# Matmul operands read alternately from two halves, in a kernel of pooled attention and two FFNs

## The chip, the cores and the metric

One core of one Trainium2 chip runs the whole program. The metric is device time in microseconds (us). Five engines work side by side: TensorE (PE; its weight loads are shown as PEld), VectorE (DVE), ScalarE (ACT), GpSimd (POOL) and SyncE (SP), which issues most of the DMAs.

## The reference

`q` is 2 x 12288 x 128, `kv` is 2 x 384 x 32 x 128, and each FFN has weights of 128 x 2048 and 2048 x 128.

```python
kv_pool = kv.reshape(B, H // 4, 4, W // 4, 4, C).mean(axis=(2, 4))   # 768 keys per batch
k = v = kv_pool.reshape(B, -1, C) @ w_sr
s = (q @ k.transpose(0, 2, 1)) / sqrt(C)
a = softmax(s)
x = (a @ v).reshape(B * 12288, C)
h = x @ moe_w_in;  x = where(h > 0, h, exp(min(h, 0)) - 1) @ moe_w_out
h = maximum(x @ moe2_w_in, 0);  out = (h * h) @ moe2_w_out
```

All of it is float32.

## The kernel before, in words

The 24,576 tokens are worked off in 48 blocks of 512 (`NB`), 24 for each batch. Channels lie on the partitions and tokens along the row, so a block is the moving operand of nearly every matmul, 512 columns wide, and weights are the stationary one. Each FFN has 16 chunks of 128 hidden channels (`NF`). For full precision each operand is held as a high part and a low part (`xH`, `xL`; `wi0H`, `wi0L`), and one product takes three matmuls: weight low by operand high, high by high, high by low (`products`, lines 308 to 310).

A block t goes through these steps:

- **scores** (lines 684 to 690): four pieces of 128 tokens. The queries stand still, the keys `kH`, `kL` of the batch move, 768 columns in spans of 512 and 256. Row maximum on DVE (L707), exponential on ACT (L711), normalisation on ACT or POOL, then a 32x32 transpose on DVE (`turn`, L729) and 16 DMAs (`move`, L791) that finish the transposition into `pL`.
- **values** (`weigh`, lines 807 to 811): `pH` is cut off by ACT (L801), `pL` by DVE (L805), and six key chunks of three matmuls each give x. Blocks 0 to 2 do this with single-part operands and 128-wide matmuls (`plain_values`, L833).
- **hidden** 0 and 1 (L880): x or y against 16 weight chunks into PSUM banks. FFN 0 then has exp on ACT (L891), `less_one` on POOL (L894), `pick` on DVE (L898), the high part on ACT (L902), the low part on DVE (`gL`, L905). FFN 1 has relu and square on ACT (L923, L926), the high part on POOL (L929), the low part on DVE (`sL`, L933).
- **down** 0 and 1 (L947): the hidden channels in pairs of chunks, 16 products summed in one bank. y is split by ACT and DVE (`split`, L620, L621); the output of FFN 1 is transposed on DVE (L969) and written by four DMAs (L974), each taking 32 channels.

Matmul results lie in the order in which the moving operand is read. Before the change everything is read in the order in which it lies, and token columns stay in their order from q to the output.

The order of all instructions on all engines is made in advance by `Program.order`. Each step has an engine, a cost and a priority (its due time, in blocks of 16 x 3200). The planner walks through the costs as times, and at each point takes from an engine's queue the step that can start first, with preference by priority. After 130,000 ns of planned time costs are multiplied by `SLACK` of the engine. The table `MOVED` shifts the priority of single steps. A step's cost thus sets the order and no more; each engine on the chip works through its list and waits on semaphores.

Of the kernel before, what the change touches and what calls it, by code (L numbers as in the profile page):

```python
# [22 lines left out]
IDLE, MARGIN, FILLER, COLD, WARM = 330.0, 60.0, 224.0, 430.0, 6300.0  # L23
OPENING, EAGER = 60000.0, 250.0
BULK = 130000.0
SLACK = {"pe": 1.0, "act": 1.17, "dve": 1.1, "pool": 1.16, "sp": 1.0}
LATENCY = {"pe": 197, "act": 135, "dve": 110, "pool": 120, "sp": 2300}
SAME = {"pe": 0, "act": 110, "dve": 0, "pool": 60, "sp": 2300}
BEGIN = {"pe": 1360.0, "act": 2500.0, "dve": 900.0, "pool": 1300.0, "sp": 1800.0}

MOVED = {
    "aH": {(0, 0, 3): 3720, (0, 2, 6): 28360, (1, 1, 5): 1580},
    "aL": {(0, 2, 2): 200, (0, 3, 1): 22430, (1, 1, 3): 2340},
    "cut": {(0, 0, 1): 12280, (0, 1, 1): 18660, (1, 1, 3): 17420},
    "down": {(0, 0, 10): -7210, (0, 0, 11): -61170, (0, 0, 9): -390, (0, 1, 11): 1860, (0, 2, 3): 17140,
        (0, 2, 9): 14060, (0, 3, 0): 4990, (0, 3, 8): -7760, (1, 0, 0): -34230, (1, 0, 11): 8280, (1, 0, 2): -28660,
        (1, 1, 2): 360, (1, 1, 3): -12810},
    "exp": {(0, 5): 9510, (0, 6): 7700, (1, 14): 10480, (2, 1): 1790, (3, 12): 55960, (3, 13): 8500},
    "hidden": {(0, 0, 12): -20, (0, 0, 8): 6730, (0, 1, 13): -3490, (0, 1, 15): -360, (0, 1, 6): 7080,
# [6 lines left out]
    "high_part": {(0, 1, 0): 11700, (1, 1, 2): 20980, (1, 1, 3): 9580},  # L46
    "join": {(1, 0, 2): -10420, (1, 1, 3): -28280},
    "k_hi": {(0, 1): -90},
    "less_one": {(3, 10): -10910, (3, 14): 17140},
    "low_part": {(1, 0, 1): 18510},  # L50
    "normalise": {(3, 0): 520, (4, 2): 4360},
    "pick": {(1, 11): 12410, (2, 0): 18920, (2, 3): -14380, (2, 6): -13180, (3, 10): -8840},
    "q_transpose": {(2,): -3420},
    "recip": {(3, 3): -2180},
    "relu": {(0, 3): -10730, (0, 7): -410, (1, 15): 11630, (1, 6): -29110, (2, 8): -3270},
    "scores": {(3, 1): 4220, (4, 3): -3470},
    "turn": {(4, 1): 11280},
    "v_hi": {(0,): 24340},
    "values": {(1, 3): -13460, (2, 1): 18540, (2, 3): 7470, (3, 2): 15850},
    "xL": {(3,): -2040},  # L60
    "yH": {(3,): -19030},
}


class Program:
# [25 lines left out]

    def order(self, kinds, fill=None):

        for tag, moved in MOVED.items():
            for key, by in moved.items():
                engine, cost, priority, *rest = self.ops[(tag, *key)]
                self.ops[(tag, *key)] = (engine, cost, priority + by, *rest)
# [77 lines left out]
def kernel(  # L175
# [19 lines left out]
    nc = tc.nc  # L195
# [107 lines left out]
    def f32(t):  # L303
        return t.bitcast(F32)

    def products(dst, lhs, rhs, start=True, stop=True):

        nc.tensor.matmul(dst, lhs[1], rhs[0], start=start, stop=False)  # L308
        nc.tensor.matmul(dst, lhs[0], rhs[0], start=False, stop=False)  # L309
        nc.tensor.matmul(dst, lhs[0], rhs[1], start=False, stop=stop)  # L310
# [209 lines left out]
    def make_keys(b, due):  # L520
# [20 lines left out]
        def make(x, due):  # L541
            ps, hi, lo = (x + "ps", b), (x + "H", b), (x + "L", b)
            scale = SCALE if x == "k" else 1.0

            def chunk(c):
                dst = v_chunk(flat(buf(*ps)), c)
                keys = buf("pooled", b)[:, c * P:(c + 1) * P]
                nc.tensor.matmul(dst, *((wsr, keys) if x == "k" else (keys, wsr)), start=True, stop=True)  # L548

            def hi_half(h):  # L550
                x = spans[h]
                nc.scalar.activation(buf(*hi)[:, x], flat(buf(*ps))[:, x], AF.Copy, scale=scale)

            def lo_half(h):
                x = spans[h]
                nc.vector.scalar_tensor_tensor(
                    out=buf(*lo)[:, x], in0=flat(buf(*ps))[:, x], scalar=scale, in1=f32(buf(*hi)[:, x]),
                    op0=ALU.mult, op1=ALU.subtract,
                )

            if b == 0:
                from_near(x, due)
            for c in range(NKC if b else 0):
                op((x, b, c), "pe", 280 if x == "k" else 223, due, partial(chunk, c),
                   kept + ([(x, b, 0)] if c else []),
                   [] if c else [("scores", ps), (x + "H", hi), (x + "L", lo)],
                   last=[("pooled", b)])
            if x == "v" and b == 0:
                plain_v(due)
                return  # L570
            for h in range(2):
                op((x + "_hi", b, h), "act", 370, due, partial(hi_half, h),
                   [(x, b, h)] if b == 0 else [(x, b, c) for c in range(4 * h, min(4 * h + 4, NKC))])
                op((x + "_lo", b, h), "dve", 470, due, partial(lo_half, h), [(x + "_hi", b, h)], last=[ps])
# [22 lines left out]

    spans = (slice(0, NB), slice(NB, NKEY))

    def v_chunk(x, c):  # L600
        return x[:, c * C:(c + 1) * C]

# [3 lines left out]
    G = P // 32  # L606
    q_rows = q.rearrange("b (t g j) c -> (b t) j g c", g=NB // 32, j=32)
    q_tokens = q.rearrange("b (t s p) c -> (b t) p s c", s=NS, p=P)
    out_rows = out.rearrange("(t g j) c -> t j g c", g=NB // 32, j=32)

    def pieces(x, a):
        return x[32 * a:32 * (a + 1), :].rearrange("p (g i) -> p g i", i=32)
# [14 lines left out]
    def attention(t, base):  # L627
# [53 lines left out]
        def softmax(s, due):  # L681
            k = (t, s)

            def scores():
                x = [a[:, s * P:(s + 1) * P] for a in parts("qT", t)]
                ps, kH, kL = flat(buf("scores", *k)), buf("kH", b), buf("kL", b)
                for y in spans:
                    nc.tensor.matmul(ps[:, y], x[0], kH[:, y], start=True, stop=False)  # L688
                    nc.tensor.matmul(ps[:, y], x[0], kL[:, y], start=False, stop=False)  # L689
                    nc.tensor.matmul(ps[:, y], x[1], kH[:, y], start=False, stop=True)  # L690

            def span_scores(h):
                x, y = [a[:, s * P:(s + 1) * P] for a in parts("qT", t)], spans[h]
# [102 lines left out]
        def weigh(j, due):  # L796
# [10 lines left out]
            def values():  # L807
                vH, vL = buf("vH", b), buf("vL", b)
                for i in range(2 * j, 2 * j + 2):
                    products(buf("xps", t), (v_chunk(vH, i), v_chunk(vL, i)),  # L810
                             [buf(x, t)[:, i, :] for x in ("pH", "pL")], start=(i == 0), stop=(i == NKC - 1))

            if t >= EARLY:
                op(("p_hi", *k), "act", 945, due, p_hi, [("move", t)] + ([("p_hi", t, 0)] if j else []),
# [3 lines left out]
            if j == NKC // 2 - 1:  # L818
                done = [("pH", t), ("pL", t)]
                if t % BPB == BPB - 1:  # L820
                    done += [("vH", b), ("vL", b)]
            op(("values", *k), "pe", 1364, due, values,
               ([("p_lo", *k)] if t >= EARLY else [("p_lo", t, s) for s in range(NS)])
               + ([("v_lo", b)] if b == 0 else [("v_lo", b, 0), ("v_lo", b, 1)]) + ([("values", t, j - 1)] if j else []),
               [("bank" if t > 2 else "bank0", ("xps", t))] if j == 0 else (), last=done)
# [49 lines left out]
    def hidden(j, t, i, due):  # L875
# [1 line left out]
        x = "xy"[j]  # L877

        def fn():
            products(buf("h", *k), [w[:, i, :] for w in wi[j]], parts(x, t))  # L880

        op(("hidden", *k), "pe", 682, due, fn, [(x + "L", t), ("low_part", j, 0, i // 4)], [("bank" if t + j > 2 else "bank0", ("h", *k))],
           last=[(x + "H", t), (x + "L", t)])

    def elu(t, i, due):
# [57 lines left out]
    def down(j, t, i, due):  # L943
        pair = (j, t, i // 2)

        def fn():
            products(buf("acc", j, t), [w[:, i, :] for w in wo[j]], [buf(x, *pair)[:, i % 2, :] for x in ("aH", "aL")],  # L947
                     start=(i == 0), stop=(i == NF - 1))

        def half(h):  # L950
            x = slice(h * NB // 2, (h + 1) * NB // 2)
            products(buf("acc", j, t, h)[:, :NB // 2], [w[:, i, :] for w in wo[j]],
                     [buf(y, *pair)[:, i % 2, x] for y in ("aH", "aL")], start=(i == 0), stop=(i == NF - 1))

        after = [("aL", *pair), ("low_part", j, 1, i // 4)]
        if t == NBLK - 1 and j:
# [2 lines left out]
                   after + ([("down", j, t, i - 1, h)] if i else []),  # L959
                   () if i else [("bank", ("acc", j, t, h))], last=[("aH", *pair), ("aL", *pair)])  # L960
            return
        op(("down", j, t, i), "pe", 682, due, fn, after + ([("down", j, t, i - 1)] if i else []),
           () if i else [("bank" if t + j > 2 else "bank0", ("acc", j, t))], last=[("aH", *pair), ("aL", *pair)])

    def store(t, due):
# [3 lines left out]
            nc.vector.transpose(out=buf("o", t), in_=buf(*acc))  # L969

        def write():
            for a in range(G):
                queue = nc.scalar if t == NBLK - 1 and a % 2 else nc.sync
                queue.dma_start(out=out_rows[t, :, :, 32 * a:32 * (a + 1)], in_=pieces(buf("o", t), a))  # L974
# [15 lines left out]
                op(("o_write", t, h), "sp", 1000, due, partial(write_half, h), [("o_transpose", t, h)], last=[("o", t)])  # L990
            return
        op(("o_transpose", t), "dve", 630, due, transpose, [("down", 1, t, NF - 1)], [("o", ("o", t))], last=[acc])
        op(("o_write", t), "sp", 2000, due, write, [("o_transpose", t)], last=[("o", t)])


    for t in range(NKC):
# [72 lines left out]
```

## Time and profile before

| what | value |
|---|---|
| median of 3 runs | 2542.16 us (2542.04 to 2542.49) |
| the profiled execution | 2542.52 us, of which the span of the trace is 2540.7 us |
| busy PE / DVE / ACT / POOL | 2531.9 / 2231.3 / 2080.5 / 1308.0 us |
| granted TensorE clock | 1.00 of full speed over the span |

Matmuls are pipelined: a matmul's duration in the trace (390 ns for 512 columns) overlaps the next one's, so the rate is read from the distance between two starts. The span of one execution is some 1.8 us shorter than its time.

### The profile page before, as it was taken

The numbers are of one execution on the slowest core, as the hardware profiler recorded it, in microseconds if no ns is written. First come the engines' busy times: TensorE is split into PE (matmuls) and PEld (weight loads), VectorE is DVE, ScalarE is ACT, GpSimd is POOL, SyncE is SP. The second block draws the span as 40 slices with busy tenths as digits, with TensorE's granted clock in tenths as the row PEclk, the third lists the DMA queues.
The fourth block names the chain that finished last, engine by engine and source line by source line (L and its number), as shares of the span: only waits on it lengthen the run. The fifth ranks groups of instructions, "written<-read, shape, count | busy, mean of one in ns | idle before, by whom it ended". The sixth has DMA issues, their size and how long they took to land.

```text
span 2540.7 us, 34933 instructions
## 1 busy us (share of the span) xinstructions
PE 2531.9 (100%) x11639; PEld 2107.5 (83%) x11639; DVE 2231.3 (88%) x2725; ACT 2080.5 (82%) x3137; POOL 1308.0 (51%) x1319
## 2 busy tenths in 40 slices
PE   9999999999999999999999999999999999999999
PEld 8888888888888888888888888888888888888888
DVE  7988889889898898988898888888888989888885
ACT  6988888788888788787888888888888888888886
POOL 4654454555665455554545445554555444544553
PEclk9999999999999999999999999999999999999999
DMA  6122111222122221221112111121112111211110
GB/s 225 38 48 49 34 38 34 55 59 46 42 46 61 56 46 42 63 51 34 38 34 56 41 38 34 45 51 34 38 34 60 37 38 34 49 44 31 33 30 13
DMA packets 358853, 119.28 MB, mean 47 GB/s; under 512 B 208912, under 2 KB 352912, under 8 KB 358672
## 3 DMA queue, kind: packets, MB, share of 16 engines
q1 hardware_dynamic: 357440, 116.85, 19.2%
q8 instruction: 92, 1.51, 0.2%
q14 instruction: 89, 0.73, 0.1%
q10 hardware_dynamic: 1232, 0.20, 0.0%
HBM read 33.61 MB, written 12.58 MB: 18 GB/s over the span
## 4 chain that ended last, share of the span: by engine, by line
PE 98%; DVE 1%; DMA 0%; ACT 0%; issue 0%; SPq 0%; DVEq 0%
PE banks L308 30%; PE banks L309 30%; PE banks L310 30%; PE banks L690 3%; PE banks L689 3%; PE banks L688 3%; PE banks L833 0%; DMA gH<-in_kv_dram 0%; PE banks L462 0%; DVE sL L933 0%; PE banks L736 0%; DVE gL L905 0%; DVE g L898 0%; DVE max L707 0%; PE banks L548 0%
## 5 line engine op out<-in xcount | busy, mean ns | idle before, releaser
L894 POOL TENSOR_SCALAR e<-e 128x512 f32<-128x512 f32 x768 | 706.4, 928 | 528.9 <-ACT e L891 441.3
L929 POOL TENSOR_SCALAR sH<-r 128x1024 fp32r<-128x1024 f32 x380 | 420.0, 1105 | 628.5 <-ACT r L926 256.3
L891 ACT ACTIVATE e<-banks 128x512 f32<-128x512 f32 x768 | 459.1, 600 | 196.7 <-PE banks L310 180.3
L933 DVE TENSOR_TENSOR sL<-r,sH 128x1024 fp32r<-128x1024 f32 x380 | 550.7, 1449 | 59.5 <-POOL sH L929 59.4
L905 DVE TENSOR_TENSOR gL<-g,gH 128x1024 fp32r<-128x1024 f32 x384 | 518.2, 1351 | 77.3 <-ACT gH L902 74.4
L923 ACT ACTIVATE r<-banks 128x512 f32<-128x512 f32 x768 | 458.9, 599 | 113.9 <-PE banks L310 98.8
L898 DVE SCALAR_TENSOR_TENSOR g<-e,banks 128x512 f32<-128x512 f32 x768 | 501.3, 671 | 24.0 <-POOL e L894 20.8
L902 ACT CAST gH<-g 128x1024 fp32r<-128x1024 f32 x384 | 401.9, 1047 | 14.2 <-DVE g L898 10.5
L926 ACT ACTIVATE r<-r 128x1024 f32<-128x1024 f32 x384 | 407.7, 1062 | 6.9
L308 PE MATMUL banks<-yH,wi1L 128*128 128x512 f32 x768 | 300.1, 391 | 0.2
L308 PE MATMUL banks<-xH,wi0L 128*128 128x512 f32 x768 | 300.1, 391 | 0.0
L308 PE MATMUL banks<-gH,wo0L 128*128 128x512 f32 x768 | 299.7, 390 | 0.0
L309 PE MATMUL banks<-yH,wi1H 128*128 128x512 f32 x768 | 299.4, 390 | 0.0
L309 PE MATMUL banks<-gH,wo0H 128*128 128x512 f32 x768 | 299.4, 390 | 0.0
L309 PE MATMUL banks<-xH,wi0H 128*128 128x512 f32 x768 | 299.2, 390 | 0.0
L310 PE MATMUL banks<-xL,wi0H 128*128 128x512 f32 x768 | 298.9, 389 | 0.0
L310 PE MATMUL banks<-yL,wi1H 128*128 128x512 f32 x768 | 298.8, 389 | 0.0
L310 PE MATMUL banks<-gL,wo0H 128*128 128x512 f32 x768 | 298.8, 389 | 0.0
L310 PE MATMUL banks<-sL,wo1H 128*128 128x512 f32 (+1 forms) x768 | 297.4, 387 | 1.0 <-DVE sL L933 1.0
L308 PE MATMUL banks<-sH,wo1L 128*128 128x512 f32 (+1 forms) x768 | 297.8, 388 | 0.0
L309 PE MATMUL banks<-sH,wo1H 128*128 128x512 f32 (+1 forms) x768 | 297.4, 387 | 0.0
L711 ACT ACTIVATE prob<-banks,max 128x768 f32<-128x768 f32 x191 | 172.3, 902 | 49.5 <-DVE max L707 46.4
(181 smaller groups left out, 4327.9 us busy)
## 6 DMA issues: line engine op xcount, KB each, us to landing
pL<-turned SPq DMA_DIRECT2D x720, 96.0 KB, 2.2
out_dram<-o SPq DMA_DIRECT2D x188, 64.0 KB, 1.9
q<-in_q_dram SPq DMA_DIRECT2D x180, 64.0 KB, 2.3
ld<-in_kv_dram SPq DMA_DIRECT2D x24, 256.0 KB, 3.6
ld<-in_kv_dram SPq DMA_DIRECT2D x4, 512.0 KB, 5.5
g<-in_kv_dram SPq DMA_DIRECT2D x4, 512.0 KB, 6.3
gH<-in_kv_dram SPq DMA_DIRECT2D x3, 512.0 KB, 7.8
r<-in_moe_w_in_dram SPq DMA_DIRECT2D x3, 511.8 KB, 6.9
```

Of the source, the lines that this page charges most:

```text
L308: nc.tensor.matmul(dst, lhs[1], rhs[0], start=start, stop=False)
L309: nc.tensor.matmul(dst, lhs[0], rhs[0], start=False, stop=False)
L310: nc.tensor.matmul(dst, lhs[0], rhs[1], start=False, stop=stop)
L891: nc.scalar.activation(buf("e", *k), buf(*h), AF.Exp)
L894: nc.gpsimd.tensor_scalar(out=buf("e", *k), in0=buf("e", *k), scalar1=-1.0, scalar2=1.0, op0=ALU.add, op1=ALU.mult)
L898: nc.vector.scalar_tensor_tensor(out=buf("g", *pair)[:, i % 2, :], in0=buf("e", *k), scalar=0.0, in1=buf(*h), op0=ALU.min, op1=ALU.max)
L902: nc.scalar.copy(buf("aH", 0, *pair), buf("g", *pair))
L905: nc.vector.tensor_sub(buf("aL", 0, *pair), buf("g", *pair), f32(buf("aH", 0, *pair)))
L923: nc.scalar.activation(buf("r", *pair)[:, i % 2, :], buf(*h), AF.Relu)
L926: nc.scalar.activation(buf("r", *pair), buf("r", *pair), AF.Square)
L929: nc.gpsimd.tensor_scalar(out=buf("aH", 1, *pair), in0=buf("r", *pair), scalar1=1.0, scalar2=1.0, op0=ALU.mult, op1=ALU.mult)
L933: nc.vector.tensor_sub(buf("aL", 1, *pair), buf("r", *pair), f32(buf("aH", 1, *pair)))
```

## The change

Every FFN product and every value product of the blocks from 3 on now reads its moving operand through `paired`: columns 0, 256, 1, 257, and so on, so two neighbouring reads lie 256 columns (1024 bytes) apart. The result lies in the order read. Values, hidden 0, down 0, hidden 1 and down 1 each shuffle the tokens once, and the write to memory takes the accumulated order into account (`out_rows`; blocks 0 to 2, whose values aren't shuffled, use `out_early` and eight DMAs instead of four).

The score matmuls read their keys alternately too: in batch 0 within each span (256 apart in the span of 512, 128 apart in that of 256), in batch 1 over all 768 columns, 384 apart. `kH` and `kL` are written in such places that the scores come out in the old order.

In the planner the cost of a hidden or down step goes from 682 to 648 and that of a value step from 1364 to 1296. `SLACK` is lowered for DVE and POOL, a new table `AFTER` shifts whole kinds of steps in the blocks from 3 on, and `MOVED` has other entries. So the order changes on every engine.

```diff
-SLACK = {"pe": 1.0, "act": 1.17, "dve": 1.1, "pool": 1.16, "sp": 1.0}
+SLACK = {"pe": 1.0, "act": 1.17, "dve": 1.085, "pool": 1.09, "sp": 1.0}
+AFTER = {("aH", 1): 8560, ("aL", 0): 1530, ("aL", 1): -9360, ("down", 1): -1890, "exp": -5170,
+         ("hidden", 0): 520, ("hidden", 1): 500, "less_one": 4410, "o_transpose": -5280, "p_hi": 10050,
+         "p_lo": -1040, "pick": -2620, "recip": -3590, "scores": -6800, "turn": 25890, "xL": 7740}
 MOVED = {
-    "aH": {(0, 0, 3): 3720, (0, 2, 6): 28360, (1, 1, 5): 1580},
+    "aH": {(1, 1, 0): 12060, (1, 1, 1): 5250},
...
     def order(self, kinds, fill=None):
+        for name, (engine, cost, priority, *rest) in self.ops.items():
+            if priority > -9e5 and len(name) <= 4:
+                staged = name[0] in ("hidden", "down", "aH", "aL")
+                block = name[1 + staged] if len(name) > 1 + staged else 0
+                if block >= 3:
+                    priority += AFTER.get(name[:2] if staged else name[0], 0)
+                    self.ops[name] = (engine, cost, priority, *rest)
...
+    def paired(x):
+        return x.rearrange("p (a b) -> p b a", a=2)
...
+            def place(y, h):
+                return of_span(b, y, h) if x == "k" else two(y[:, spans[h]])
             def hi_half(h):
-                nc.scalar.activation(buf(*hi)[:, x], flat(buf(*ps))[:, x], AF.Copy, scale=scale)
+                nc.scalar.activation(place(buf(*hi), h), two(flat(buf(*ps))[:, spans[h]]), AF.Copy, scale=scale)
...
+    def of_span(b, x, h):
+        if b:
+            return paired(x)[:, NB // 2 * h:min(NB // 2 * (h + 1), NKEY // 2), :]
+        return paired(x[:, spans[h]])
+
+    def two(x):
+        return x.rearrange("p (b a) -> p b a", a=2)
...
-    out_rows = out.rearrange("(t g j) c -> t j g c", g=NB // 32, j=32)
+    out_rows = out.rearrange("(t j g) c -> t j g c", g=NB // 32, j=32)
+    out_early = out.rearrange("(t k g e) c -> t e k g c", g=NB // 32, k=16, e=2)
...
-                for y in spans:
-                    nc.tensor.matmul(ps[:, y], x[0], kH[:, y], start=True, stop=False)
-                    nc.tensor.matmul(ps[:, y], x[0], kL[:, y], start=False, stop=False)
-                    nc.tensor.matmul(ps[:, y], x[1], kH[:, y], start=False, stop=True)
+                for h, y in enumerate(spans):
+                    hi, lo = of_span(b, kH, h), of_span(b, kL, h)
+                    nc.tensor.matmul(ps[:, y], x[0], hi, start=True, stop=False)
+                    nc.tensor.matmul(ps[:, y], x[0], lo, start=False, stop=False)
+                    nc.tensor.matmul(ps[:, y], x[1], hi, start=False, stop=True)
...
                     products(buf("xps", t), (v_chunk(vH, i), v_chunk(vL, i)),
-                             [buf(x, t)[:, i, :] for x in ("pH", "pL")], start=(i == 0), stop=(i == NKC - 1))
+                             [paired(buf(x, t)[:, i, :]) for x in ("pH", "pL")], start=(i == 0), stop=(i == NKC - 1))
...
-            products(buf("h", *k), [w[:, i, :] for w in wi[j]], parts(x, t))
-        op(("hidden", *k), "pe", 682, due, fn, [(x + "L", t), ("low_part", j, 0, i // 4)], [("bank" if t + j > 2 else "bank0", ("h", *k))],
+            products(buf("h", *k), [w[:, i, :] for w in wi[j]], [paired(y) for y in parts(x, t)])
+        op(("hidden", *k), "pe", 648, due, fn, [(x + "L", t), ("low_part", j, 0, i // 4)], [("bank" if t + j > 2 else "bank0", ("h", *k))],
...
-            products(buf("acc", j, t), [w[:, i, :] for w in wo[j]], [buf(x, *pair)[:, i % 2, :] for x in ("aH", "aL")],
+            products(buf("acc", j, t), [w[:, i, :] for w in wo[j]], [paired(buf(x, *pair)[:, i % 2, :]) for x in ("aH", "aL")],
...
+            if t < PLAIN:
+                for a in range(G):
+                    for e in range(2):
+                        nc.sync.dma_start(out=out_early[t, e, :, :, 32 * a:32 * (a + 1)],
+                                          in_=pieces(buf("o", t), a)[16 * e:16 * (e + 1)])
+                return
```

On TensorE, where a block's values begin (block 24 of 48; `turned` and `pL` are its weights' high and low part, `kH` and `kL` the keys), before:

```order
L688 MATMUL banks<-kH_11602,qTH_12954 128x256
L689 MATMUL banks<-kL_11603,qTH_12954 128x256
L690 MATMUL banks<-kH_11602,qTL_13010 128x256
L308 MATMUL banks<-turned_13097,vL_11669 128x512
L309 MATMUL banks<-turned_13097,vH_11668 128x512
L310 MATMUL banks<-pL_12965,vH_11668 128x512
```

and at the last two values of the same block, after the change:

```order
L323 MATMUL banks<-turned_13108,vL_11734 128x512
L324 MATMUL banks<-turned_13108,vH_11733 128x512
L325 MATMUL banks<-pL_12956,vH_11733 128x512
L323 MATMUL banks<-yH_12925,wi1L 128x512
L324 MATMUL banks<-yH_12925,wi1H 128x512
L325 MATMUL banks<-yL_12936,wi1H 128x512
L323 MATMUL banks<-xH_12727,wi0L 128x512
L324 MATMUL banks<-xH_12727,wi0H 128x512
L325 MATMUL banks<-xL_12765,wi0H 128x512
L714 MATMUL banks<-kH_11629,qTH_12880 128x512
L715 MATMUL banks<-kL_11630,qTH_12880 128x512
L716 MATMUL banks<-kH_11629,qTL_13027 128x512
```

Before, a block's six value triples stand in one piece behind the scores; now they come two by two, with hidden and down products and a score step between them.

On VectorE at the same place (`pL` is the low part of the value weights, `gL` and `sL` those of the two FFNs), before:

```order
L933 TENSOR_TENSOR sL_13107<-r_13032,sH_13084 128x1024
L805 TENSOR_TENSOR pL_12965<-pL_12965,turned_13097 128x1024 x2
L905 TENSOR_TENSOR gL_13137<-g_13077,gH_13105 128x1024
L805 TENSOR_TENSOR pL_12965<-pL_12965,turned_13097 128x1024
L707 TENSOR_REDUCE max_13150<-banks 128x1
```

and now:

```order
L831 TENSOR_TENSOR pL_12956<-pL_12956,turned_13108 128x1024
L959 TENSOR_TENSOR sL_13138<-r_13050,sH_13115 128x1024
L931 TENSOR_TENSOR gL_13151<-g_13076,gH_13122 128x1024
L831 TENSOR_TENSOR pL_12956<-pL_12956,turned_13108 128x1024
L733 TENSOR_REDUCE max_13166<-banks 128x1
L924 SCALAR_TENSOR_TENSOR g_13120<-e_13132,banks 128x512
L831 TENSOR_TENSOR pL_12956<-pL_12956,turned_13108 128x1024
L959 TENSOR_TENSOR sL_13198<-r_13103,sH_13177 128x1024
L931 TENSOR_TENSOR gL_13209<-g_13120,gH_13186 128x1024
```

The three `pL` steps stood close together and now have a pair of FFN steps between them; `sL` and `gL` come one behind the other.

## Rows read from the trace of the kernel before

**Rows 1.** The page's span and its busy times with shares and instruction counts.

```profile
span 2540.7 us, 34933 instructions
PE 2531.9 (100%) x11639; PEld 2107.5 (83%) x11639; DVE 2231.3 (88%) x2725; ACT 2080.5 (82%) x3137; POOL 1308.0 (51%) x1319
```

**Rows 2.** The page's chain that ended last, shares by engine.

```profile
PE 98%; DVE 1%; DMA 0%; ACT 0%; issue 0%; SPq 0%; DVEq 0%
```

**Rows 3.** All waits of PE: for whom, us in total, times, longest.

```profile
PE banks L1031 <- POOL ident masks.py:199: 1.4, 1, 1.4
PE banks L688 <- DVE turned L746: 1.1, 1, 1.1
PE banks L310 <- DVE sL L933: 1.0, 1, 1.0
...
PE banks L833 <- DVE turned L746: 0.2, 1, 0.2
```

**Rows 4.** PE's timeline by start (us): FFN matmuls, then scores.

```profile
1395.81 0.39 PE L308 MATMUL banks<-gH,wo0L 128*128 128x512 f32 x1
1396.04 0.39 PE L309 MATMUL banks<-gH,wo0H 128*128 128x512 f32 x1
1396.27 0.39 PE L310 MATMUL banks<-gL,wo0H 128*128 128x512 f32 x1
...
1403.29 0.39 PE L688 MATMUL banks<-kH,qTH 128*128 128x512 f32 x1
...
1403.97 0.28 PE L688 MATMUL banks<-kH,qTH 128*128 128x256 f32 x1
...
1404.33 0.40 PE L308 MATMUL banks<-turned,vL 128*128 128x512 f32 x1
```

**Rows 5.** PE's groups by line and form: count, busy, mean ns.

```profile
L308 PE MATMUL banks<-xH,wi0L 128*128 128x512 f32 x768 | 300.1, 391 | 0.0
L310 PE MATMUL banks<-sL,wo1H 128*128 128x512 f32 x752 | 292.9, 389 | 1.0 <-DVE sL L933 1.0
L308 PE MATMUL banks<-turned,vL 128*128 128x512 f32 x270 | 105.8, 392 | 0.0
L688 PE MATMUL banks<-kH,qTH 128*128 128x512 f32 x188 | 73.6, 392 | 1.1 <-DVE turned L746 1.1
L688 PE MATMUL banks<-kH,qTH 128*128 128x256 f32 x188 | 52.2, 278 | 0.0
```

**Rows 6.** A stretch of 200 us: busy and counts by engine, then clock, DMA.

```profile
core 0: us, PE busy (x) PEld busy (x) DVE busy (x) ACT busy (x) POOL busy (x), PEclk, DMA share, GB/s
1400.00:1600.00 200.00, 200.00 (x906) 166.30 (x904) 179.87 (x219) 166.16 (x250) 97.68 (x99) 1.00 0.17 38
```

**Rows 7.** PE's timeline in the opening: two matmuls in plain float32.

```profile
16.82 1.02 PE L658 MATMUL banks<-qT,red 128*128 128x512 f32 x2
17.68 0.38 PE L462 MATMUL banks<-o,g 128*128 128x128 f32 x2
```

**Rows 8.** DVE's groups by line and form: busy, mean ns, idle before.

```profile
L933 DVE TENSOR_TENSOR sL<-r,sH 128x1024 fp32r<-128x1024 f32 x380 | 550.7, 1449 | 59.5 <-POOL sH L929 59.4
L354 DVE SCALAR_TENSOR_TENSOR e<-r,e 128x512 uint32<-128x512 uint32 x2 | 1.4, 678 | 0.0
L457 DVE TENSOR_TENSOR gH<-gH 128x512 f32<-128x512 f32 x2 | 1.4, 692 | 0.5 <-DMA gH<-in_kv_dram 0.5
L556 DVE SCALAR_TENSOR_TENSOR kL<-banks,kH 128x512 fp32r<-128x512 f32 x2 | 1.4, 684 | 1.1 <-ACT kH L552 1.1
```

**Rows 9.** SP's timeline around an output write: issue times in us.

```profile
143.86 2.19 SPq L636 DMA_DIRECT2D q<-in_q_dram  x4
161.34 1.96 SPq L974 DMA_DIRECT2D out_dram<-o  x4
183.59 10.32 SPq L791 DMA_DIRECT2D pL<-turned  x16
```

More of the change, by code (lines that the diff above doesn't have):

```diff
@@ L29 @@
 BEGIN = {"pe": 1360.0, "act": 2500.0, "dve": 900.0, "pool": 1300.0, "sp": 1800.0}
+AFTER = {("aH", 1): 8560, ("aL", 0): 1530, ("aL", 1): -9360, ("down", 1): -1890, "exp": -5170,
+         ("hidden", 0): 520, ("hidden", 1): 500, "less_one": 4410, "o_transpose": -5280, "p_hi": 10050,
+         "p_lo": -1040, "pick": -2620, "recip": -3590, "scores": -6800, "turn": 25890, "xL": 7740}
 MOVED = {
-    "aH": {(0, 0, 3): 3720, (0, 2, 6): 28360, (1, 1, 5): 1580},
-    "aL": {(0, 2, 2): 200, (0, 3, 1): 22430, (1, 1, 3): 2340},
@@ L34 @@
[L34 to L39, printed above, removed]
[6 rows of a table removed]
@@ L46 @@
[L46 to L61, printed above, removed]
+    "aH": {(1, 1, 0): 12060, (1, 1, 1): 5250},
+    "aL": {(0, 2, 5): 14860, (0, 3, 7): 2230, (0, 4, 1): -15440, (1, 1, 0): 7790, (1, 1, 2): 8410},
+    "cut": {(0, 1, 0): -41650},
+    "down": {(0, 1, 10): 360, (0, 1, 11): 3120, (0, 1, 7): -21830, (0, 1, 9): -34650, (0, 2, 0): -11550,
+        (0, 2, 12): -10550, (0, 2, 15): -19040, (0, 2, 4): 2060, (0, 3, 8): 73460, (1, 0, 1): -10000,
+        (1, 0, 11): -7140, (1, 0, 15): -10410, (1, 0, 3): -10890, (1, 0, 6): -24480, (1, 1, 0): 2660,
+        (1, 1, 2): 5540},
@@ new lines @@
+    "exp": {(3, 13): -29550, (3, 15): -1510},
+    "exps": {(2, 0): -39560, (4, 3): 45250, (5, 3): 22370},
+    "fold": {(1, 0, 2): 8060},
+    "hidden": {(0, 1, 1): -5070, (0, 1, 12): 5960, (0, 1, 15): 6630, (0, 2, 1): 1740, (0, 2, 10): 4140,
[7 rows of a table added]
+    "join": {(0, 1, 2): 7160, (0, 1, 3): -16850},
+    "k_lo": {(0, 0): 23080},
+    "less_one": {(0, 7): -9610, (1, 8): 2630, (3, 9): -27910, (4, 1): -11320},
+    "low_part": {(0, 1, 3): 24890},
+    "normalise": {(1, 0): 42460, (3, 0): 4950},
+    "p_hi": {(3, 0): -4080, (4, 1): 5000, (4, 2): 670},
@@ new lines @@
+    "p_lo": {(4, 2): -16470},
+    "pick": {(1, 0): 41710, (2, 15): 13160, (3, 15): -12810, (3, 5): 34510, (4, 5): -12910},
+    "recip": {(2, 1): 3250, (3, 2): 3020, (4, 2): 23200},
+    "relu": {(0, 1): -4570, (1, 0): -14160, (1, 1): -8810, (1, 2): 4410, (2, 2): -15030, (2, 7): 11550},
+    "scores": {(2, 0): -2380, (3, 0): 3090, (4, 2): 7970, (4, 3): 8200, (5, 3): 24570},
+    "square": {(0, 4): 4000, (2, 1): -33900},
+    "v_hi": {(0,): -2040},
+    "values": {(1, 0): -5220, (2, 0): 2940},
@@ L62 @@
+    "yL": {(2,): -14940},
 }
@@ L548, in chunk @@
                 nc.tensor.matmul(dst, *((wsr, keys) if x == "k" else (keys, wsr)), start=True, stop=True)
+            def place(y, h):
+                return of_span(b, y, h) if x == "k" else two(y[:, spans[h]])
             def hi_half(h):
-                x = spans[h]
-                nc.scalar.activation(buf(*hi)[:, x], flat(buf(*ps))[:, x], AF.Copy, scale=scale)
+                nc.scalar.activation(place(buf(*hi), h), two(flat(buf(*ps))[:, spans[h]]), AF.Copy, scale=scale)
             def lo_half(h):
-                x = spans[h]
                 nc.vector.scalar_tensor_tensor(
-                    out=buf(*lo)[:, x], in0=flat(buf(*ps))[:, x], scalar=scale, in1=f32(buf(*hi)[:, x]),
+                    out=place(buf(*lo), h), in0=two(flat(buf(*ps))[:, spans[h]]), scalar=scale, in1=place(f32(buf(*hi)), h),
                     op0=ALU.mult, op1=ALU.subtract,
@@ L821, in weigh @@
                     done += [("vH", b), ("vL", b)]
-            op(("values", *k), "pe", 1364, due, values,
+            op(("values", *k), "pe", 1296, due, values,
                ([("p_lo", *k)] if t >= EARLY else [("p_lo", t, s) for s in range(NS)])
@@ L946, in fn @@
         def fn():
-            products(buf("acc", j, t), [w[:, i, :] for w in wo[j]], [buf(x, *pair)[:, i % 2, :] for x in ("aH", "aL")],
+            products(buf("acc", j, t), [w[:, i, :] for w in wo[j]], [paired(buf(x, *pair)[:, i % 2, :]) for x in ("aH", "aL")],
                      start=(i == 0), stop=(i == NF - 1))
         def half(h):
-            x = slice(h * NB // 2, (h + 1) * NB // 2)
+            x = slice(h * NB // 4, (h + 1) * NB // 4)
             products(buf("acc", j, t, h)[:, :NB // 2], [w[:, i, :] for w in wo[j]],
-                     [buf(y, *pair)[:, i % 2, x] for y in ("aH", "aL")], start=(i == 0), stop=(i == NF - 1))
+                     [paired(buf(y, *pair)[:, i % 2, :])[:, x, :] for y in ("aH", "aL")], start=(i == 0), stop=(i == NF - 1))
         after = [("aL", *pair), ("low_part", j, 1, i // 4)]
@@ L961, in down @@
             return
-        op(("down", j, t, i), "pe", 682, due, fn, after + ([("down", j, t, i - 1)] if i else []),
+        op(("down", j, t, i), "pe", 648, due, fn, after + ([("down", j, t, i - 1)] if i else []),
            () if i else [("bank" if t + j > 2 else "bank0", ("acc", j, t))], last=[("aH", *pair), ("aL", *pair)])
@@ L992, in store @@
         op(("o_transpose", t), "dve", 630, due, transpose, [("down", 1, t, NF - 1)], [("o", ("o", t))], last=[acc])
-        op(("o_write", t), "sp", 2000, due, write, [("o_transpose", t)], last=[("o", t)])
+        op(("o_write", t), "sp", 4000 if t < PLAIN else 2000, due, write, [("o_transpose", t)], last=[("o", t)])
     for t in range(NKC):
```

13 rows, old and new, of the table MOVED are left out of this document.

## The prediction

> **What bounds the kernel now.** I read the busy times first. PE is busy for 2531.9 of 2540.7 us, DVE for 2231.3 (88%), ACT for 82%, POOL for 51% [rows 1]. A busy PE can be a PE that crawls, so the next view is the chain of waits, followed back from the end: 98% of it is PE [rows 2]. The third is PE's own waits: the longest is 1.4 us, and only one, of 1.0 us, is for a result of the FFN loop (`sL`) [rows 3]. So from the opening to the last block PE never waits, and only three things can shorten the time: fewer matmuls, faster matmuls, or a shorter opening and tail. The change leaves the number of matmuls as it is.
>
> The rate is read from starts. From 1395.81 to 1403.29 us there are 33 matmuls of 512 columns, 7.48 us or 226.7 ns each [rows 4]. [...]
>
> [...]
>
> **The change part by part.**
>
> 1. *FFN and value products, and the 512-wide part of the scores, read alternately.* Count: nine groups of 768 and three of 752 for the FFNs, three of 270 for the values, three of 188 for the scores [rows 5] (one line of each kind): 6912 + 2256 + 810 + 564 = 10,542 matmuls. At 226.7 ns they fill 2390 us. No row shows a moving operand read in two places, so the new rate is bounded. Below: 213.3 ns, no cycle lost, a gain of 13.4 x 10,542 = 141 us. Above: plain float32 matmuls of 512 columns, the slowest stream in the trace, take (17.68 - 16.82) / 2 = 430 ns [rows 7], a loss of 203 x 10,542 = 2143 us. I take 216 ns. [...] The planner's new cost says the same (648 / 3 = 216); its old one (682 / 3 = 227.3) is what the trace shows, but the new one is a claim that no row of before bears out. Gain: 10.7 x 10,542 = 113 us.
>
> 2. *The 256-wide scores.* 3 x 188 = 564 matmuls [rows 5] at 120 ns or less. [...] They already run at more than 226.7 / 2, so I take no change. The last block's 96 half-wide down matmuls go with them.
>
> 3. *The other order.* It issues the same 2727 DVE, 2952 ACT and 1324 POOL instructions. PE's cover for it was the slack of the others. In the stretch of 200 us DVE is busy for 179.87, ACT for 166.16 [rows 6]. That stretch holds about 860 wide matmuls; 10.7 ns from each makes it 190.8 us, and the same work then fills DVE to 94% and ACT to 87%. DVE's idle time falls from 20.1 to 10.9 us in such a stretch. Nothing of before shows DVE above 90% over so long a stretch, so waits of PE are bounded by 0 (nearly what before has [rows 3]) and by a DVE that can't pass 92%: 179.87 / 0.92 = 195.5 us, which is 4.7 us per stretch or about 58 us over the 2475 us or so of steady work. I take 6 us, near the row of before, because the moves go the right way: values come two by two between FFN products, so that the three `pL` steps of DVE aren't due at once, and `sL` and `gL` are made in pairs as PE uses them. What is late first is `sL`: it takes 1449 ns on average, and POOL's `sH` ends the wait before it [rows 8]. If it is late, the down products behind it on PE wait, and with them everything in PE's list.
>
> 4. *Keys written to alternating places.* Four steps on ACT and four on DVE in the whole program, two of each wide, 684 ns for a wide one on DVE [rows 8]. Doubled, the DVE steps would cost some 2 us in all, half of it in the opening; bound 0 to 3 us with ACT's share (reads and counts stay, so no gain), taken as 0. If the cover were gone, batch 1's first scores would be late by that.
>
> 5. *The writes of blocks 0 to 2.* Twelve more DMA issues on SP at 1.96 / 4 = 0.49 us, 6 us, in a queue that stands empty for 15 us and more on either side of a write [rows 9]. Behind them stand q loads and moves that are planned blocks ahead. Taken as 0, at most 6. All later writes keep their count and their pieces of 32 channels.
>
> 6. *PE's opening* has three more filler matmuls of 128 columns, under 1 us; taken as 0.
>
> Sum, made against the profiled execution's 2542.5 us (span 2540.7 [rows 1] and 1.8 around it; the median of the runs is 0.4 lower): 2542.5 - 113 + 6 = 2435.5, against the median 2435.
>
> **The rivals.**
>
> *A. DVE becomes the bound.* The matmuls get faster as in step 1, but DVE, with its fused steps of 1.4 us that wait for POOL and ACT in turn, doesn't pass 92%. For it: 90% in the stretch of 200 us already [rows 6], and every tenth of a microsecond that `sL` (1449 ns) takes longer beside a busier POOL costs 38 us of DVE time. Against: half of DVE's present idle time exists only because PE is slow to hand over. Time: 2542 - 113 + 58 = 2487. PE's waits would then be many, for `sL`, `gL` and freed banks.
>
> *B. It does not do what it says.* [...] Time: 2542 give or take 3; only the order would act.
>
> *C. Slower: each alternate read costs.* [...] It decides as soon as the spacing is above 226.7 ns. [...] In the trace two DVE steps speak to it weakly: L354 reads one operand in steps of 8 bytes and takes 678 ns, L457 reads runs of neighbours and takes 692 [rows 8], so there a step costs nothing. 1024 bytes are not 8, and DVE is not PE.
>
> [...]
>
> **How the numbers follow.** Forecast (216 ns or somewhat off it, few waits): 0.70, its own range 2402 (no cycle lost, no waits: 2542.5 - 141) to 2460. Rival A, 2460 to 2530: 0.11. Rival B: 0.07. Rival C: 0.12. The range 2402 to 2500 holds the forecast and most of A, 0.79. Two runs of this kernel can be told apart at about 0.2%, 5 us; faster than that is the forecast and A, 0.81; within it is B, 0.07; slower is C, 0.12.
>
> **What would show it.** Right: starts of neighbouring 512-wide FFN matmuls 216 ns apart, at a granted clock of 1.00; the stretch of 200 us with some 950 matmuls instead of 906, DVE at 94%; PE's waits a few us in total. Wrong in step 1: a spacing of 213 or 222. Wrong in step 3: waits of PE for `sL`, `gL` or `pL` of tens of us. Scores that go another way than FFN matmuls would say that the distance between the two places matters. Wrong altogether: a spacing of 227 or more.

## The result and the profile after

The changed kernel takes 2419.1 us (2418.95 to 2419.13) against 2542.1 us before in the same series: ratio 0.9516, 95% interval 0.9499 to 0.9532. It is faster, as forecast, inside the range, and 16 us below the predicted 2435.

The page of the changed kernel, span and busy times; they answer to [rows 1]:

```profile
span 2417.3 us, 34913 instructions
PE 2408.2 (100%) x11645; PEld 2121.6 (88%) x11645; DVE 2165.0 (90%) x2725; ACT 2075.4 (86%) x3137; POOL 1311.5 (54%) x1319
```

PE is still what bounds the kernel. DVE has the same number of instructions and 66 us less busy time.

PE's timeline of the changed kernel, by start in us: FFN matmuls, then scores, to be read beside [rows 4].

```profile
1395.12 0.38 PE L323 MATMUL banks<-sH,wo1L 128*128 128x512 f32 x1
1395.34 0.38 PE L324 MATMUL banks<-sH,wo1H 128*128 128x512 f32 x1
...
1397.06 0.27 PE L714 MATMUL banks<-kH,qTH 128*128 128x256 f32 x1
...
1397.40 0.38 PE L323 MATMUL banks<-xH,wi0L 128*128 128x512 f32 x1
...
1403.22 0.38 PE L714 MATMUL banks<-kH,qTH 128*128 128x512 f32 x1
```

From 1397.40 to 1403.22 there are 27 wide matmuls (512 columns), 215.6 ns each, where before took 226.7. The three narrow score matmuls (256 columns) take 113 ns each, where before took 120. Averaged over all starts after 130 us, wide FFN and value matmuls went from 227.3 to 215.9 ns, narrow scores from 117.5 to 111.0.

The 200 us that stand in [rows 6], in the changed kernel (busy and counts by engine, clock, DMA):

```profile
1400.00:1600.00 200.00, 200.00 (x951) 176.22 (x950) 180.48 (x231) 173.31 (x262) 110.29 (x108) 1.00 0.19 43
```

951 matmuls instead of 906, at the same granted clock of 1.00. DVE is busy for 90% of the stretch (93% of the 200 us from 100 on, 91% from 1100 on), not for the 94% that I had worked out; ACT is at 87%, as worked out.

PE's longest waits, answering to [rows 3], and DVE's `sL` group, answering to [rows 8]:

```profile
PE banks L1063 <- POOL ident masks.py:199: 1.4, 1, 1.4
PE banks L859 <- ACT turned L770: 0.8, 2, 0.5
PE banks L665 <- DVE g L924: 0.7, 1, 0.7
```

```profile
L959 DVE TENSOR_TENSOR sL<-r,sH 128x1024 fp32r<-128x1024 f32 x380 | 496.8, 1307 | 45.1 <-POOL sH L955 45.0
```

No wait of PE after the opening blocks stands among the three longest, and `sL` takes 1307 ns where it took 1449.

### The profile page after: what moved, and what is told of

It is laid out like the page before. It is cut to its first block, busy times and chain, and to the rows that moved or that the text cites. A ratio compares the mean times of both kernels' runs of the same rounds, so it can differ in the third digit from the quotient of the medians.

```text
span 2417.3 us, 34913 instructions
## 1 busy us (share of the span) xinstructions
PE 2408.2 (100%) x11645; PEld 2121.6 (88%) x11645; DVE 2165.0 (90%) x2725; ACT 2075.4 (86%) x3137; POOL 1311.5 (54%) x1319
## 4 chain that ended last, share of the span: by engine, by line
PE 98%; DVE 1%; ACT 0%; DMA 0%; issue 0%; POOL 0%; SPq 0%; DVEq 0%; ACTq 0%
PE banks L323 30%; PE banks L324 30%; PE banks L325 30%; PE banks L715 3%; PE banks L716 3%; PE banks L714 2%; PE banks L859 1%; DMA gH<-in_kv_dram 0%; DVE g L924 0%; PE banks L477 0%; DVE gL L931 0%; DVE yH L369 0%; PE banks L762 0%; PE banks L563 0%; PE banks L1063 0%
## 5 line engine op out<-in xcount | busy, mean ns | idle before, releaser
L920 POOL TENSOR_SCALAR e<-e 128x512 f32<-128x512 f32 x768 | 751.2, 982 | 666.3 <-ACT e L917 655.0
L955 POOL TENSOR_SCALAR sH<-r 128x1024 fp32r<-128x1024 f32 x380 | 402.9, 1060 | 365.5 <-PE banks L324 107.9
L959 DVE TENSOR_TENSOR sL<-r,sH 128x1024 fp32r<-128x1024 f32 x380 | 496.8, 1307 | 45.1 <-POOL sH L955 45.0
L323 PE MATMUL banks<-xH,wi0L 128*128 128x512 f32 x768 | 292.1, 380 | 0.2 <-DVE g L924 0.2
L323 PE MATMUL banks<-yH,wi1L 128*128 128x512 f32 x768 | 291.8, 380 | 0.0
L324 PE MATMUL banks<-gH,wo0H 128*128 128x512 f32 x768 | 291.4, 379 | 0.0
L324 PE MATMUL banks<-xH,wi0H 128*128 128x512 f32 x768 | 291.4, 379 | 0.0
L324 PE MATMUL banks<-yH,wi1H 128*128 128x512 f32 x768 | 291.4, 379 | 0.0
L323 PE MATMUL banks<-sH,wo1L 128*128 128x512 f32 (+1 forms) x768 | 289.9, 377 | 0.0
L733 DVE TENSOR_REDUCE max<-banks 128x1 f32<-128x768 f32 x188 | 177.7, 945 | 23.9 <-PE banks L716 23.8
```

What stands on the lines that cost most here:

```text
L920: nc.gpsimd.tensor_scalar(out=buf("e", *k), in0=buf("e", *k), scalar1=-1.0, scalar2=1.0, op0=ALU.add, op1=ALU.mult)
L955: nc.gpsimd.tensor_scalar(out=buf("aH", 1, *pair), in0=buf("r", *pair), scalar1=1.0, scalar2=1.0, op0=ALU.mult, op1=ALU.mult)
L959: nc.vector.tensor_sub(buf("aL", 1, *pair), buf("r", *pair), f32(buf("aH", 1, *pair)))
```

## The experiments

**The two halves of the change apart.** First the new order alone: of the changed kernel the reads are put back, in FFN, values and scores, with the output written to suit.

```diff
     def paired(x):
-        return x.rearrange("p (a b) -> p b a", a=2)
+        return x
...
-    out_rows = out.rearrange("(t j g) c -> t j g c", g=NB // 32, j=32)
+    out_rows = out.rearrange("(t g j) c -> t j g c", g=NB // 32, j=32)
```

> The changed kernel with its new order on every engine, but every moving operand read in a row, and the output written accordingly. Theory 1 (all of the gain is the reading): 2542, within 5 us. Theory 2 (the 16 us by which the result beat the forecast come from the better order): 2526 to 2535. PE's waits under 10 us by both.

It took 2539.7 us, ratio to before 0.9991 (0.9981 to 1.0). Theory 1 holds: the order alone is worth 2.4 us, hardly more than the noise, and between this kernel and the changed one, which differ in the reads only, lie 120.6 us. The 2.4 us have a counterpart in the traces: counted over all starts after 130 us, 23 matmuls of before start more than 260 ns behind the one ahead, 3.7 us beyond 216 ns each, and 9 of this kernel, 0.9 us.

Then the reads alone, in the old order (with before's costs, `SLACK` and `MOVED`; the diff is against the changed kernel):

```diff
-SLACK = {"pe": 1.0, "act": 1.17, "dve": 1.085, "pool": 1.09, "sp": 1.0}
+SLACK = {"pe": 1.0, "act": 1.17, "dve": 1.1, "pool": 1.16, "sp": 1.0}
-AFTER = {("aH", 1): 8560, ("aL", 0): 1530, ("aL", 1): -9360, ("down", 1): -1890, "exp": -5170,
...
+AFTER = {}
```

> The kernel before with its old order, costs and tables, but alternate reads everywhere (and the eight small writes in blocks 0 to 2). Theory 1 (the reading is all, DVE keeps up in any order): 2419 to 2425, waits of PE under 6 us. Theory 2 (the new order is what lets DVE keep up): 2435 to 2490, with waits of PE for sL, gL or pL of 15 us or more.

It took 2432.3 us, ratio 0.9569 (0.9553 to 0.9585): neither theory. The reads bring 109.8 us by themselves, and then the order is worth 13.2 us, which it isn't while the reads are slow. The waits of PE's weight loads (which stand ahead of its matmuls) in this kernel, and in the changed one, longest first:

```profile
PEld banks L318 <- ACT r L944: 6.5, 17, 1.2
PEld banks L318 <- DVE g L919: 5.8, 14, 0.8
PEld banks L320 <- DVE sL L954: 3.7, 4, 1.5
```

```profile
PEld banks L323 <- DVE g L924: 1.7, 4, 0.5
PEld banks L859 <- ACT turned L770: 1.4, 2, 0.9
```

In the old order PE waits for banks that ACT and DVE are to free (L318 is the first matmul of a product) and for `sL`. By the same count 66 matmuls start more than 260 ns behind the one ahead, 12.7 us beyond 216 ns each; in the changed kernel 11, 1.0 us. So waits account for 11.7 of the 13.2 us. One of the 66 in the old order, PE's, DVE's and POOL's timelines:

```profile
672.15 0.38 PE L319 MATMUL banks<-sH,wo1H 128*128 128x512 f32 x1
673.66 0.48 PE L320 MATMUL banks<-sL,wo1H 128*128 128x512 f32 x1 [1.13 <-DVE sL L954]
```

```profile
670.41 1.22 DVE L926 TENSOR_TENSOR gL<-g,gH 128x1024 fp32r<-128x1024 f32 x1
671.55 2.06 DVE L954 TENSOR_TENSOR sL<-r,sH 128x1024 fp32r<-128x1024 f32 x1
```

```profile
670.75 1.78 POOL L950 TENSOR_SCALAR sH<-r 128x1024 fp32r<-128x1024 f32 x1 [1.71 <-PE banks L319]
```

`sL` takes 2.06 us here and PE stands for 1.1 us. It begins while POOL works on the `sH` of another pair, until 672.53, and ends 1.08 us after that. Over the run it takes 1440 ns in the old order (1449 before), and 1307 to 1318 ns in the new one, with fast reads or slow:

```profile
L954 DVE TENSOR_TENSOR sL<-r,sH 128x1024 fp32r<-128x1024 f32 x380 | 547.4, 1440 | 39.1 <-POOL sH L950 38.8
```

```profile
L957 DVE TENSOR_TENSOR sL<-r,sH 128x1024 fp32r<-128x1024 f32 x380 | 500.7, 1318 | 55.3 <-POOL sH L953 55.2
```

So the shorter `sL` belongs to the order. What makes it long shows in the traces. When no POOL step is running as `sL` begins, it takes 1.21 to 1.22 us on average, in every kernel. When one is running, mostly `less_one` (tile `e`), it takes about 1.6 us in the old order (1.49 in the changed kernel) and, in all but 6 of 677 cases, ends 1.06 to 1.2 us after that POOL step. In the old order 217 of the 380 begin so (220 with fast reads), in the new one 114 with slow reads and 126 with fast. The kernel of TensorE beside other engines, further down, has the same subtraction of 128x1024 by itself, and then beside ACT, POOL and DMAs:

```profile
L68 DVE TENSOR_TENSOR d<-d,d 128x1024 fp32r<-128x1024 f32 x15 | 18.4, 1225 | 0.5
```

```profile
L68 DVE TENSOR_TENSOR d<-d,d 128x1024 fp32r<-128x1024 f32 x14 | 21.2, 1516 | 0.4
```

Beside ACT alone it stays at 1225 ns, and all 14 subtractions of the second row begin while a POOL step is running. How much of the 13.2 us the shorter `sL` is worth, apart from the rest of the order, was not measured; most of the waits are for banks.

**The scores alone put back.** The same undoing in `of_span` and `place` only.

```diff
     def of_span(b, x, h):
-        if b:
-            return paired(x)[:, NB // 2 * h:min(NB // 2 * (h + 1), NKEY // 2), :]
-        return paired(x[:, spans[h]])
+        return x[:, spans[h]]
```

> The changed kernel with the scores' keys read in a row and stored in the old order, all else as changed. Theory 1: 564 wide score matmuls lose 11 ns each, 564 of 256 columns lose 4 to 8 ns, 6.2 + 3.6 = 10 us, so 2429. Rival (the first matmuls after the short ones are those that were slow before, so a disturbance spreads into the FFN matmuls): up to 2435. Rival (scores don't matter because PE then waits for DVE's row maximum): 2419 to 2422.

2430.4 us, ratio 0.956 (0.9546 to 0.9574), 11.3 us above the changed kernel: theory 1 in size. Both rivals are out: the FFN and value matmuls stay at 215.9 ns on average, and the time is not near 2422. PE's timeline of this kernel at one score step:

```profile
1397.36 0.40 PE L712 MATMUL banks<-kH,qTH 128*128 128x512 f32 x1
1397.60 0.40 PE L713 MATMUL banks<-kL,qTH 128*128 128x512 f32 x1
...
1398.06 0.28 PE L712 MATMUL banks<-kH,qTH 128*128 128x256 f32 x1
...
1398.42 0.38 PE L323 MATMUL banks<-turned,vL 128*128 128x512 f32 x1
1398.63 0.38 PE L324 MATMUL banks<-turned,vH 128*128 128x512 f32 x1
```

The three wide score matmuls take 233 ns each (231.1 on average after 130 us, 226.8 in the kernel with all reads in a row), more than the 226.7 of a long series in a row, and the alternating matmul behind them is at 0.21 at once: a disturbance stays with the reads in a row. So some 2 of the 11.3 us come from mixing the two ways of reading, and the scores themselves are worth some 9: over the 528 of each width after 130 us, 5.8 in the wide ones (226.8 to 215.9 ns) and 3.4 in the narrow (117.5 to 111.0).

**TensorE by itself.** A kernel of nothing but series of 64 matmuls, one per way of reading, run once. High-part float32 is the type in which the kernel holds high and low parts (`fp32r` where steps write it; the rows of matmuls say f32 for it and for plain float32). In [rows 4] 512 columns in a row take 226.7 ns and 256 take 120: the 256 more cost 106.7 ns, 0.417 each. 512 columns at that price would be 213.3, so a wide matmul loses 13.4 ns, as long as 32 columns, or the time of one column in every 16. That time is the cycle of the theories here.

```diff
+    for i in range(N):  # in a row
+        nc.tensor.matmul(bank(i, 512), weights(i), row, start=True, stop=True)
+    for i in range(N):  # 256 apart
+        nc.tensor.matmul(bank(i, 512), weights(i), ways(2), start=True, stop=True)
```

> TensorE alone: series of 64 matmuls (128x128 by 128x512 in high-part float32), each series reading its moving operand in another way; nothing of the reference is computed. Theory 1 (the lost cycles belong to reading neighbouring columns: one cycle each time the reader leaves a piece of 16 columns, hidden when two pieces are read by turns): in a row 226.7 ns from start to start, also with one weight and one column further on; 256, 384, 512, 1024 apart 216; distances of 128 down to 16 also 216; 8, 4 and 2 apart, where both reads lie in one piece, 227; four, eight, sixteen places 216; every 2nd, 4th, 8th and 16th column of a single stream 240, 267, 320, 427. [...] Theory 3 (different banks are what helps): some distances, above all large powers of two, stay at 227 or more while others reach 216.

A row of PE's timeline is one series; the distance of two starts over 64 is the price of a matmul.

```profile
24.45 14.67 PE L53 MATMUL banks<-src,w 128*128 128x512 f32 x64
38.95 13.98 PE L55 MATMUL banks<-src,w 128*128 128x512 f32 x64
52.77 13.98 PE L57 MATMUL banks<-src,w 128*128 128x512 f32 x64
...
177.81 13.98 PE L75 MATMUL banks<-src,w 128*128 128x512 f32 x64
191.63 14.71 PE L77 MATMUL banks<-src,w 128*128 128x512 f32 x64
206.17 18.26 PE L79 MATMUL banks<-src,w 128*128 128x512 f32 x64
224.27 31.41 PE L81 MATMUL banks<-src,w 128*128 128x512 f32 x64
...
283.24 29.05 PE L85 MATMUL banks<-src,w 128*128 128x512 f32 x64
312.11 29.62 PE L87 MATMUL banks<-src,w 128*128 128x512 f32 x64
341.55 27.77 PE L89 MATMUL banks<-src,w 128*128 128x512 f32 x64
```

In a row (L53) 226.7 ns, 256 apart (L55) 215.8, and the same 215.8 at distances of 1024, 512, 384, 257, 128, 64, 32, 16, 8 and 4 (L75). At 2 apart (L77) it is 227 again, with four places (L79) 283, eight (L81) 488. With sixteen places it is 433. A single stream of every 2nd column takes 451 (L85), of every 4th 460 (L87), of every 8th 431 (L89), and one in a row that starts one column further on 237. Theory 1 is right on distances of 16 and more, and wrong elsewhere: 8 and 4 apart lie within 16 columns and still take 215.8, and it had more than two places at 216, every 2nd to every 8th column at 240 to 320 and the shifted start at 226.7. Theory 3 is out.

**Fewer moving columns, fewer weights.** Is the loss one of columns or one of matmuls?

```diff
+    for i in range(N):  # 256 columns in a row
+        nc.tensor.matmul(banks[:128, i % 4, :256], cols(i, 128), src[:, :256], start=True, stop=True)
+    for i in range(N):  # in a row, 64 weight columns
+        nc.tensor.matmul(banks[:64, i % 4, :512], cols(i, 64), row, start=True, stop=True)
```

> TensorE alone again, nothing of the reference is computed: series of 64 matmuls with fewer moving columns, fewer weight columns, and weights read in steps. Theory S (streaming: a cycle lost per 16 moving columns): 448, 384, 320, 256, 192 columns in a row take 198, 170, 142, 113, 85 ns, the number of weight columns and their step change nothing. [...]

Rows as above, 384 columns in a row (L81) and half apart (L83), 320 (L87, L89), 256 (L93, L95):

```profile
176.32 11.27 PE L81 MATMUL banks<-src,w 128*128 128x384 f32 x64
187.43 10.56 PE L83 MATMUL banks<-src,w 128*128 128x384 f32 x64
...
208.92 9.55 PE L87 MATMUL banks<-src,w 128*128 128x320 f32 x64
218.31 8.86 PE L89 MATMUL banks<-src,w 128*128 128x320 f32 x64
...
236.38 7.85 PE L93 MATMUL banks<-src,w 128*128 128x256 f32 x64
244.07 7.31 PE L95 MATMUL banks<-src,w 128*128 128x256 f32 x64
251.22 7.45 PE L97 MATMUL banks<-src,w 128*64 128x256 f32 x64
```

In a row 173.6, 146.7 and 120.2 ns. From 320 to 512 columns (146.7 to 226.7 ns) a further column costs 0.417 ns, as in [rows 4], and over that price (160.0, 133.3, 106.7) stand 13.4 to 13.6 ns, as with 512 columns; 448 columns take 202.8, 16.1 over. Theory S had 170, 142 and 198 ns for 384, 320 and 448 columns and is out: the loss does not shrink with the width. Alternately 162.5 and 135.8, 2.5 over.

At 256 columns the test is not clean: alternately they stay at 111.7, which is also what 192 columns take either way, and with 64 weight columns (L97) 256 in a row take 113.8, near theory S, and 192 take 89. So a floor that goes with the weight columns stands under the narrow ones.

Fewer weights do not take the loss away: 512 in a row take 230 with 64 weight columns and 232 with 32, no less. With every 2nd weight column they take 234 in a row and 216 alternately, with every 4th 235 and 237: there alternate reading gains nothing. What takes the 13.4 ns stays open, and so does why alternate reads get back 10.9 of them. Two, four, eight and sixteen neighbours by turns from two places took 340, 250, 243 and 240: only single columns by turns pay.

**Where it holds.** The last series: starts, banks, and other types.

```diff
+    for i in range(N):  # bfloat16 256 apart
+        nc.tensor.matmul(banks[:, i % 4, :512], wb[:, P * (i % 4):P * (i % 4 + 1)], half[:, :512].rearrange("p (a b) -> p b a", a=2), start=True, stop=True)
```

> TensorE alone, nothing of the reference is computed: what else could make or hide the 13.4 ns that a matmul reading in a row loses whatever its width. [...]

Starts 128 to 6144 columns on, and one, two or four result banks, all 226.7, and weights out of the same tile 227: the loss stays with all of these. Starts of 4 and 16 columns on take 232 and 229 on average. bfloat16 (L98 in a row, L100 and L102 alternately, 256 and 8 apart):

```profile
365.19 13.98 PE L98 MATMUL banks<-half,wb 128*128 128x512 bf16 x64
379.00 31.16 PE L100 MATMUL banks<-half,wb 128*128 128x512 bf16 x64
410.00 31.24 PE L102 MATMUL banks<-half,wb 128*128 128x512 bf16 x64
440.62 15.15 PE L104 MATMUL banks<-src,w 128*128 128x512 f32 x64
```

In a row 215.8 ns; alternately 484 and 486, more than twice as long. A plain float32 matmul stands in the trace as two passes, and each goes from 429 ns in a row to 540 alternately, 858 to 1080 for the matmul. 5 apart in the kernel's type took 240 for 510 columns, 6 apart 212.5 for 504 (from the series before). So alternate reading helps this one type, and harms the other two.

**Four apart, in the whole kernel.**

```diff
+    def near_pairs(x):
+        return x.rearrange("p (o a b) -> p o b a", a=2, b=4)
...
-            products(buf("h", *k), [w[:, i, :] for w in wi[j]], [paired(y) for y in parts(x, t)])
+            products(buf("h", *k), [w[:, i, :] for w in wi[j]], [near_pairs(y) for y in parts(x, t)])
```

> The changed kernel, but FFN and value products read their columns 4 apart (0, 4, 1, 5, 2, 6, 3, 7, 8, ...) in place of 256 apart; the output is written as in the changed kernel, so within groups of eight tokens its rows stand in another order. [...] Rival (in the whole kernel the halves, 1024 bytes apart, matter): over 2430.

2418.1 us, ratio 0.9512 (0.9496 to 0.9527), 1 us from the changed kernel and far from the rival's 2430. For FFN and value products the halves are not needed.

**Other engines beside it.** 8% of the wide matmuls before took 230 to 237 ns, and none after (counted after 130 us).

```diff
+            for i in range(17):
+                nc.scalar.activation(a1, a1, AF.Copy)
```

> TensorE reads one tile in a row or alternately, 96 matmuls each, with nothing beside it, then beside ACT copies, DVE subtractions, POOL scalings, DMAs within SBUF, and mixtures; nothing of the reference is computed. In the kernel before, 8% of the wide matmuls took 230 to 237 ns in place of 227, after the change none do. Theory 1 (other engines' work in SBUF disturbs reading in a row): in a row 227 with nothing, 229 to 235 beside the engine that is to blame (ACT above all, by what ran beside the slow ones), 216 to 217 in alternate reading throughout. Theory 2 (the long ones come from the kernel's own PE stream, after score matmuls): 227 and 216 in every series.

Theory 1 fell and theory 2 holds in the main: beside ACT, DVE, POOL, DMAs or all four, reading in a row took 227.0 ns on average, alternating 215.8. The long ones are the first seven matmuls of a series in a row behind one of another kind (238, 224, 231, 236, 228, 233, 231, then 227), with nothing beside as well, as the series of TensorE by itself show. In the kernel before, the first five wide matmuls behind score matmuls took 233, 236, 228, 232 and 231 ns on average. Alternate reads have hardly such a start: in the changed kernel the first one behind score matmuls takes 218 ns, all others 216.

## Why the prediction came out

*Step 1 (113 us) holds in size.* FFN and value products gained 109.3 us (2539.7 - 2430.4), some 111.5 without the 2 us that the mixing of reads took back, where 9978 of the 10,542 matmuls at 10.7 ns were to bring 106.8. The chip took 215.9 ns where I took 216, which was the planner's cost, and as far as a reason of mine goes, luck. No run shows the 213.3 ns of the lower bound, and with it the 141 us and the 2402 of the range: 512 columns took 215.8 at the least, 2.5 over 0.417 ns a column. The loss does not shrink with the width (13.4 to 13.6 ns on 512, 384 and 320 columns); what rival B had wrong is that the change leaves all of it: alternate reads get back 10.9 of the 13.4 ns. My upper bound was also misread: the 430 ns of plain float32 are one of two passes, and the matmul took 860.

*Step 2 (no change for narrow scores) was too low.* The scores gained 11.3 us in all, against the 6.0 that step 1 had for their wide part. The narrow ones fell from 117.5 to 111.0 ns on average, some 3.7 us for 564 of them, though I had taken no change for them; the rest is the mixing of reads in the kernel compared with.

*Step 3 (6 us of waits) failed, and is the largest part of the 16 us.* I took DVE's work as a constant of the program and its share as 94%. The order changed the work's length: fewer `sL` begin beside a POOL step, `sL` fell to 1307 ns, 54 us over 380 of them, and DVE was at 90%. That is the term mis-sized: in place of 6 us of waits to add, the order gave back 2.4 us with slow reads, 8.4 us in all; the reads make up 7.6 more (120.6 for 113). The danger was real, only not for this order: with the old one the fast reads cost 13.2 us more, nearly all of it waits, a small case of rival A (DVE busy for 2203.5 of 2429.9 us, 91%), far from its 58.

*Steps 4 to 6 (key writes, twelve more DMAs, fillers), taken as 0,* were not measured one by one. The kernels in between share the measured gain out as 2.4 + 109.3 + 11.3 us, and whatever these steps cost is contained in that.

*Rival C* is out for the kernel's type: two places by turns are faster (215.8 ns) than one row read out (226.7). It holds for the other types (bfloat16 484 ns against 215.8 in a row, a pass of plain float32 540 against 429), and in the kernel's own for four and eight places (283 and 488). It was right to give C a chance, and the type decides.

## What to carry to other kernels

Where PE bounds a kernel and its matmuls run in this high-part float32, take the distance of two starts at two widths: what a matmul takes beyond its columns at the price of a further one (13.4 ns over 0.417 a column here) can come from the order in which the moving operand is read (10.9 of the 13.4 here), and that is free to change, since the result can be put right in a later read or in the write to memory. Try it for the type at hand, with one series of 64 matmuls: what saves 5% here takes more than twice as long in bfloat16 (484 ns against 215.8). And when the bounding engine gets faster, work out the others' load for the new order, since their steps' lengths change with what runs beside them: here VectorE's subtractions of 128x1024 with GpSimd's steps (1.21 us with none running, 1.49 to 1.63 begun beside one).

## What the runs showed of the hardware that was not expected

- High-part float32, 512 columns: 226.7 ns in a row, 215.8 alternately at the distances tried from 4 to 1024 columns save one (5 apart: 240 for 510 columns), 227 at 2, 283 from four places, 237 in a row if the start is one column off.
- The loss in a row, over 0.417 ns a column, is 13.4 to 13.6 ns per matmul for 320, 384 and 512 columns alike, 16 for 448. With every 4th weight column alternate reading gains nothing (235 and 237).
- bfloat16 has no such loss (215.8 in a row) and takes 484 alternately; a pass of plain float32 takes 429 and 540, a matmul two passes.
- A series in a row settles over its first seven matmuls or so (up to 238 ns); an alternate one has hardly such a start.
- Other engines and DMAs at work in SBUF did not slow either way of reading (227.0 and 215.8 ns).
- A VectorE subtraction of 128x1024 takes 1.21 to 1.23 us by itself or beside ScalarE. Begun while a GpSimd step is running, it ended 1.06 to 1.2 us after that step in 671 of 677 cases, up to 2.1 us in all.
